# Masking inside the score operands, heads of a pair one after the other, staging in halves, narrow last blocks and a lag of 4 steps in an attention and feed-forward kernel

## The chip, the core and the metric

The kernel runs on one core of a Trainium2 chip. The metric is the device time of one execution in microseconds. The core has five engines that work side by side, each through its own queue in order: PE (TensorE, matrix multiply; the loading of its weights is listed apart as PEld), DVE (VectorE), ACT (ScalarE), POOL (GpSimd) and SP (SyncE), which here issues nearly all DMA transfers. SBUF is the on-chip memory, PSUM the memory that PE writes its results to. Partitions are the 128 rows of both.

## The reference

Block-causal attention over 8 batches, 8 heads, 576 positions and a head size of 64, and then a two-layer feed-forward part with a rational function between the layers:

```python
B, H, S, D = q.shape                        # 8, 8, 576, 64
scores = (1 / np.sqrt(D)) * np.matmul(q, k.transpose(0, 1, 3, 2))
mask = (pos[:, None] // 64) >= (pos[None, :] // 64)
scores = np.where(mask, scores, -1000000000.0)
scores = scores - np.max(scores, axis=-1, keepdims=True)
attn = np.exp(scores)
attn = attn / (np.sum(attn, axis=-1, keepdims=True) + 1e-09)
attn_out = np.matmul(attn, v)
x = attn_out.transpose(0, 2, 1, 3).reshape(B * S, H * D)       # 4608 x 512
h = x @ w_in                                                   # 512 x 2048
P = a[0] + a[1] * h + a[2] * h * h + a[3] * h * h * h
Q = 1.0 + np.abs(b[0]) * np.abs(h) + np.abs(b[1]) * h * h
out = (P / (Q + 1e-6)) @ w_out                                 # 2048 x 512
```

Everything is float32.

## The kernel before

**Precision by splitting.** Operands are split into a high part h, rounded to PE's reduced float32 type (F32R), and a low part l, the rest. A product is then two or three matmuls: h times h, h times l, l times h.

**Attention** goes over 32 pairs of heads (`visits`), each with five query tiles t of 64, 128, 128, 128, 128 rows (`NQ`, `Q0`). Tile t sees `NK[t]` = 64, 192, 320, 448, 576 keys, and only for its last 64 keys is part of the rows masked. The steps for a pair:

- `load` brings q, k, v of the pair; `prep(p, which)` transposes q (which = 0) and k (which = 1) on PE (L354, tile `tp`), in two halves of 288 positions each; ACT writes the high part (L358) and DVE the low part (L359) into one tile `hl` for q and k. When k is done, three transfers per head (L368 to L370) put the four parts into the operand tile `kq` of that head, 128 partitions high: head j's own 64 partitions hold qh, kh, kl and the other 64 hold ql, kh, kl. A product over 128 partitions therefore gives (qh + ql) times kh.
- `scores` (L402) makes the two matmuls of a piece (L420 with kh, L421 with kl, both with the same stationary operand) into a PSUM bank of pool `ps_a`, which has five banks. For t > 0 a third matmul (L424, 64 columns, operands `mrow` and `mcol`) adds -2^30 to the first 64 rows of the last 64 keys. DVE then takes the row maximum (L425).
- `expo` (L431) does the exponential with the row sum on ACT (L437). After the second head it normalises the tile: POOL adds 1e-9 to the sums (`rc`, L444), DVE inverts, POOL multiplies the first 64 keys of both heads into `pk` (L446) and the others in place (L450).
- `transp` (L454) transposes the normalised blocks of 64 x 2 or 128 keys on PE (L469); ACT and DVE split them into high and low tiles (`pt0`, `pt1`, `pt2`; L474, L475). `pv` (L478) multiplies them with the split v (L488): 5 blocks for the query tiles 0 to 2 and 9 blocks for 3 and 4, three matmuls per block, each 256 columns wide (320 for the first block). The result goes to memory (`xscr`, L493).

**Feed-forward** (class `Ffn`) works in chunks of 256 tokens and half the hidden units at a time: phase 0 (10 of 16 blocks of hidden units) runs between the steps of the attention, phase 1 behind it. A unit has 24 matmuls of 256 columns (L200), a chain on ACT, POOL and DVE (L207 to L233), and 12 matmuls of 512 columns (L249).

**The order of work.** `attn_steps` goes over a list `items` of (pair, tile, head), one per step and ten per pair; before the change the two heads of a tile follow each other: (t0, head 0), (t0, head 1), (t1, head 0) and so on. Each step puts its follow-ups at later steps: `expo` one step later (`ALAG2`), `transp` of a tile 9 steps after its second head's scores (`ALAG3` is 10, and one less than the distance to the same tile of the next pair is taken), `pv` a step after that, and for the next pair `load` at step 0, `prep` of q at step 3 and of k at step 5 (`OFFS`). After each step, units of feed-forward work are issued by a pace that starts at step 40 + `LAST`, `LAST` being `ALAG3` + 3. A list scheduler of the language then puts the instructions of each engine into a final order, by its own estimate of when they can run; that final order is what each engine's queue holds. A matmul that waits therefore holds up all that stands behind it on PE, and a transfer that waits holds up all behind it on SP.

The buffers around the change: `kq` has three tiles for the two heads of a pair (`KQB`), the probability tiles `p` one per query tile, `pk` two, `raw` q and k one each.

Of the kernel before, what the change touches and what calls it, by code (L numbers as in the profile page):

```python
# [29 lines left out]
KQB = 3  # L30
XB = 3
HOLD = 6
ALAG3 = 10
OFFS = {5:(0,3,5)}
# [24 lines left out]
def attn_ffn_kernel(  # L59
# [238 lines left out]
    with ExitStack() as actx:  # L298
# [5 lines left out]
        pt1 = [apers.tile([128, 4, 256], F32R, name=f"pt1{x}") for x in "hl"]  # L304
        pt2 = [apers.tile([128, 9, 256], F32R, name=f"pt2{x}") for x in "hl"]

        vpad = [apers.tile([128, 128 + 4 * 192], F32R, name=f"vp{x}") for x in "hl"]
        for x in pt1:
            nc.vector.memset(x[:, 2:4, 0:128].bitcast(F32), 0.0)
        for x in pt2:  # L310
            nc.vector.memset(x[:, 7:9, 0:128].bitcast(F32), 0.0)
        for x in vpad:
            nc.vector.memset(x.bitcast(F32), 0.0)

# [28 lines left out]
        def prep(p, which):  # L343

            s = st_[p]
            if which == 0:
                s["hl"] = att.tile([128, 4, S], F32R, name=f"hl{p}", tag="hl", bufs=1)
            raw, sc = (s["qr"], s["kr"])[which], (QSCALE, 1.0)[which]
            hl = s["hl"]
            h, l = (hl[:, 0], hl[:, 3]) if which == 0 else (hl[:, 1], hl[:, 2])  # L350
            for half in range(2):
                ps = bank(p - 1, f"tp{p}_{which}_{half}")[:, :3 * LP].rearrange("p (c t) -> p c t", c=3)
                for c in range(3):
                    nc.tensor.transpose(ps[:, c, :], raw[:, half * 3 + c].rearrange("p j d -> p (j d)"),  # L354
                                        ident[:LP, :LP])
                cs = slice(half * 288, half * 288 + 288)
                pf = ps.rearrange("p c t -> p (c t)")
                nc.scalar.activation(out=h[:, cs], in_=pf, func=AF.Copy, scale=sc)  # L358
                nc.vector.scalar_tensor_tensor(out=l[:, cs], in0=pf, scalar=sc, in1=h[:, cs].bitcast(F32),  # L359
                                               op0=ALU.mult, op1=ALU.subtract)  # L360
            if which == 1:


                for j in range(2):
                    kq = att.tile([128, 3, S], F32R, name=f"kq{p}_{j}", tag="kq", bufs=KQB)
                    src = hl[64 * j:64 * j + 64].bitcast(F32)
                    other = kq[64 - 64 * j:128 - 64 * j].bitcast(F32)
                    nc.sync.dma_start(out=kq[64 * j:64 * j + 64].bitcast(F32), in_=src[:, 0:3])  # L368
                    nc.sync.dma_start(out=other[:, 1:3], in_=src[:, 1:3])
                    nc.sync.dma_start(out=other[:, 0], in_=src[:, 3])  # L370
                    s["kq", j] = kq
# [30 lines left out]
        def scores(p, t, j):  # L402
            s = st_[p]
            nq = NQ[t]
            if j == 0:
                pt = att.tile([128, 2, NK[t]], F32, name=f"p{p}_{t}", tag=f"p{t}", bufs=1)

                pk = att.tile([128, 2, 64], F32, name=f"pk{p}_{t}", tag="pk", bufs=2) if t > 0 else pt
                nm = att.tile([128, 2, 2], F32, name=f"nm{p}_{t}", tag="nm", bufs=4)
                sm = att.tile([128, 2, 2], F32, name=f"sm{p}_{t}", tag="sm", bufs=4)  # L410
                s[t] = (pt, pk, nm, sm)
# [207 lines left out]
```

## Time and profile before

| | |
|---|---|
| three runs | 1387.34, 1393.5, 1398.72 us; median 1393.5 us |
| profiled execution, its own time | 1388.67 us |
| its span, first to last instruction | 1386.9 us |
| mean granted TensorE clock | 0.971 of full speed |
| busy: PE, PEld | 1296.0 us (93%), 1190.8 us (86%) |
| busy: DVE, ACT, POOL | 1031.0 (74%), 909.3 (66%), 958.3 us (69%) |
| DMA | 200.93 MB in 225635 packets, SP's queue 53.8% of 16 engines' span |
| feed-forward's matmuls, L200 and L249 | 25% and 25% of the chain that ended last |

How to read it: busy times of PE overlap between neighbouring matmuls, so the cost of one matmul is read from the distance of the starts and not from its duration. A row of the table by stretches gives the stretch, its length, the busy time of PE, PEld, DVE, ACT and POOL with the number of instructions, the granted clock, the share of the DMA engines and GB/s. A row of waits gives the engine and the line that waited, what it waited for, the total in us, how often, and the longest.

### The profile page before, as it was taken

The numbers are of one execution on the slowest core, as the hardware profiler recorded it, in microseconds if no ns is written. First come the engines' busy times: TensorE is split into PE (matmuls) and PEld (weight loads), VectorE is DVE, ScalarE is ACT, GpSimd is POOL, SyncE is SP. The second block draws the span as 40 slices with busy tenths as digits, with TensorE's granted clock in tenths as the row PEclk, the third lists the DMA queues.
The fourth block names the chain that finished last, engine by engine and source line by source line (L and its number), as shares of the span: only waits on it lengthen the run. The fifth ranks groups of instructions, "written<-read, shape, count | busy, mean of one in ns | idle before, by whom it ended". The sixth has DMA issues, their size and how long they took to land.

```text
span 1386.9 us, 25820 instructions
## 1 busy us (share of the span) xinstructions
PE 1296.0 (93%) x8736; PEld 1190.8 (86%) x8736; DVE 1031.0 (74%) x2048; ACT 909.3 (66%) x2250; POOL 958.3 (69%) x1240
## 2 busy tenths in 40 slices
PE   4778799999899989999999999999989999999998
PEld 3667788999888889888989999999979999999897
DVE  5898877787678868877767777766756677777665
ACT  5766766777577766776777777776545655555553
POOL 4888987687677757777767676766556655556564
PEclk9687999999999999999999999999999999999999
DMA  9778555666556665675654565651711333333332
GB/s 221 191 195 236 147 150 160 168 168 181 147 136 154 163 167 140 156 171 140 168 134 110 153 149 126 150 141 44 263 55 61 107 122 122 122 122 122 122 122 91
DMA packets 225635, 200.93 MB, mean 145 GB/s; under 512 B 132064, under 2 KB 195552, under 8 KB 225504
## 3 DMA queue, kind: packets, MB, share of 16 engines
q1 hardware_dynamic: 225440, 199.28, 53.8%
q8 instruction: 70, 1.15, 0.3%
q14 instruction: 61, 0.50, 0.1%
q0 software_dynamic: 64, 0.00, 0.0%
HBM read 98.57 MB, written 44.04 MB: 103 GB/s over the span
## 4 chain that ended last, share of the span: by engine, by line
PE 70%; DVE 9%; POOL 8%; ACT 5%; DMA 4%; issue 2%; SPq 1%; POOLq 0%; ACTq 0%; DVEq 0%
PE h L200 25%; PE o L249 25%; PE o L488 9%; PE t L469 4%; PE s L420 3%; PE s L421 3%; PE tp L354 2%; ACT p L437 1%; DVE v L224 1%; POOL u L210 1%; DVE nm L425 1%; POOL p L450 1%; DMA x<-xscr 1%; POOL gl L233 1%; DVE u L223 1%
## 5 line engine op out<-in xcount | busy, mean ns | idle before, releaser
L200 PE MATMUL h<-x,wih 128*128 128x256 f32 x2304 | 442.6, 288 | 10.1 <-DMA x<-xscr 5.9
L200 PEld LDWEIGHTS h<-x,wih 128*128 128x128 f32 x2304 | 368.8, 192 | 19.6 <-issue 6.8
L200 PE MATMUL h<-x,wil 128*128 128x256 f32 x1152 | 329.5, 286 | 0.0
L249 PE MATMUL o<-woh,gl 128*128 128x512 f32 x576 | 233.0, 405 | 8.1 <-POOL gl L233 6.8
L209 POOL TENSOR_SCALAR v<-u,bab 128x512 f32<-128x512 f32 x144 | 119.7, 831 | 162.9 <-ACT u L207 160.8
L249 PE MATMUL o<-woh,gh 128*128 128x512 f32 x576 | 228.5, 397 | 0.0
L249 PE MATMUL o<-wol,gh 128*128 128x512 f32 x576 | 227.2, 395 | 0.0
L233 POOL TENSOR_TENSOR gl<-s,gh 128x512 fp32r<-128x512 f32 x144 | 188.4, 1309 | 51.4 <-ACT gh L232 48.3
L425 DVE TENSOR_REDUCE nm<-s 128x1 f32<-128x288 f32 (+4 forms) x384 | 161.7, 427 | 81.2 <-PE s L424 46.1
L200 PEld LDWEIGHTS h<-x,wil 128*128 128x128 f32 x1152 | 221.3, 192 | 0.5
L437 ACT ACTIVATE p<-s,nm 128x288 f32<-128x288 f32 (+4 forms) x384 | 184.6, 485 | 48.4 <-DVE nm L425 34.9
L210 POOL TENSOR_TENSOR u<-v,u 128x512 f32<-128x512 f32 x144 | 189.7, 1318 | 9.8
L450 POOL TENSOR_SCALAR p<-p,rc 128x128 f32<-128x128 f32 (+3 forms) x256 | 166.2, 660 | 30.0 <-DVE rc L445 28.3
L217 ACT ACTIVATE v<-u,qcb 128x512 f32<-128x512 f32 x144 | 104.6, 726 | 95.9 <-POOL u L210 95.1
L207 ACT ACTIVATE u<-h 128x512 f32<-128x512 f32 x144 | 86.0, 597 | 120.8 <-PE h L200 114.4
L420 PE MATMUL s<-kq 128*128 128x256 f32 (+3 forms) x384 | 138.3, 362 | 22.0 <-DMA kq<-hl 9.6
L211 DVE TENSOR_TENSOR s<-s,h 128x512 f32<-128x512 f32 x144 | 98.6, 684 | 68.7 <-ACT s L208 67.9
L249 PEld LDWEIGHTS o<-woh,gl 128*128 128x128 f32 x576 | 109.5, 190 | 28.9 <-POOL gl L233 9.3
L249 PEld LDWEIGHTS o<-wol,gh 128*128 128x128 f32 x576 | 109.1, 189 | 22.8
L249 PEld LDWEIGHTS o<-woh,gh 128*128 128x128 f32 x576 | 109.5, 190 | 16.0
L421 PE MATMUL s<-kq 128*128 128x256 f32 (+3 forms) x384 | 121.0, 317 | 0.0
L469 PE MATMUL t<-ident,p 128*128 128x128 f32 (+1 forms) x672 | 114.0, 280 | 6.2 <-DVE x L492 1.8
(105 smaller groups left out, 3031.9 us busy)
## 6 DMA issues: line engine op xcount, KB each, us to landing
kq<-hl SPq DMA_DIRECT2D x64, 432.0 KB, 4.2
x<-xscr SPq DMA_DIRECT2D x96, 256.0 KB, 3.6
kq<-hl SPq DMA_DIRECT2D x64, 288.0 KB, 5.3
xscr<-x SPq DMA_DIRECT2D x32, 320.0 KB, 4.2
qr<-in_q_dram SPq DMA_DIRECT2D x64, 144.0 KB, 2.8
kr<-in_k_dram SPq DMA_DIRECT2D x64, 144.0 KB, 2.9
kq<-hl SPq DMA_DIRECT2D x64, 144.0 KB, 4.8
pscr<-os SPq DMA_DIRECT2D x18, 512.0 KB, 3.2
```

The lines of the kernel that those rows point to most:

```text
L200: nc.tensor.matmul(h[:, j, :], lhsT=w[:, dc, fs], rhs=xs[dc // 2][:, dc % 2, hl, :], start=(dc == 0 and i == 0), stop=(dc == 3 and i == 2))
L209: nc.gpsimd.tensor_scalar(out=vt, in0=ut, scalar1=b1, scalar2=b0, op0=ALU.mult, op1=ALU.add)
L210: nc.gpsimd.tensor_tensor(out=ut, in0=vt, in1=ut, op=ALU.mult)
L233: nc.gpsimd.tensor_tensor(out=gl.rearrange("p j t -> p (j t)"), in0=st, in1=gh.rearrange("p j t -> p (j t)").bitcast(F32), op=ALU.subtract)
L249: nc.tensor.matmul(self.o[m], lhsT=g[:, j, ms], rhs=w[:, f, :], start=(u == 0 and j == 0 and i == 0), stop=(u == nu - 1 and j == 1 and i = ...
L420: nc.tensor.matmul(ps[:, :ww], lhsT=kq[:, 0, qs], rhs=kq[:, 1, c0:c0 + ww], start=True, stop=False)
L421: nc.tensor.matmul(ps[:, :ww], lhsT=kq[:, 0, qs], rhs=kq[:, 2, c0:c0 + ww], start=False, stop=not last)
L425: nc.vector.reduce_max(out=nm[:nq, j, i:i + 1], in_=ps[:nq, :w], axis=AX.X, negate=True)
L437: nc.scalar.activation(out=pt[:nq, j, c0:c0 + w], in_=banks[i][:nq, :w], func=AF.Exp, bias=nm[:nq, j, 0:1], scale=1.0, accum_out=sm[:nq, j ...
L450: nc.gpsimd.tensor_scalar(out=pt[:nq, jj, 64:n], in0=pt[:nq, jj, 64:n], scalar1=rc[:nq, jj:jj + 1], scalar2=1.0, op0=ALU.mult, op1=ALU.mult)
L469: nc.tensor.transpose(ps[:, i, :nq], src, ident[:nq, :nq])
L488: nc.tensor.matmul(o[:, s0:w], lhsT=vblock(vv, x), rhs=pp, start=(x == 0 and i == 0), stop=(x == nb - 1 and i == 2))
```

## The change

The operand tile `kq` gets a fourth plane, and the two score matmuls get a stationary and a moving operand each. The first pairs (qh, mask row part) with (kh, mask column part): the head's own 64 partitions hold qh and kh, and the other 64 hold two mask planes, which are built once on POOL, written to memory (`mscr`) and copied from there into each `kq`. The second pairs (qh, ql) with (kl, kh). The matmul with `mrow` and `mcol` is gone; the product ql times kl, which the two matmuls before included, is gone too.

`items` puts the five tiles of head 0 ahead of the five of head 1. `prep` does one half of q or k at a time, at steps 5, 6, 7 and 8, with `load` at step 3; each half has an `hl` tile of its own (two buffers) and its own transfers: four per half of q or k, and one per head for the mask planes, so 18 per pair in place of 6. `ALAG3` is 4 and always holds, so `LAST` is 7 in place of 13.

The last two blocks of each `pv` get tiles of their own (`pt3`, `pt4`), 128 columns wide, so that their matmuls are 128 wide in place of 256. The transposes of query tile 0 use all 128 rows of a tile `p0` with zeros in its lower half; those of tile 4 are grouped 4, 3, 2 in place of 3, 3, 3, and the copy and subtraction of tile 2's four blocks are split in two. `pk` has four buffers, and the maxima a tile per head.

```diff
-ALAG3 = 10
-OFFS = {5:(0,3,5)}
+ALAG3 = 4
+OFFS = {5:(3,5,6,7,8)}
...
-    mrow = cpool.tile([128, 128], F32R, name="mrow")
-    mcol = cpool.tile([128, 64], F32R, name="mcol")
...
-        pt1 = [apers.tile([128, 4, 256], F32R, name=f"pt1{x}") for x in "hl"]
-        pt2 = [apers.tile([128, 9, 256], F32R, name=f"pt2{x}") for x in "hl"]
+        pt1 = [apers.tile([128, 2, 256], F32R, name=f"pt1{x}") for x in "hl"]
+        pt2 = [apers.tile([128, 7, 256], F32R, name=f"pt2{x}") for x in "hl"]
+        pt3, pt4 = ([apers.tile([128, 2, 128], F32R, name=f"pt{i}{x}") for x in "hl"] for i in (3, 4))
+        p0 = apers.tile([128, 2, 64], F32, name="p0")
+        nc.vector.memset(p0[64:128], 0.0)
...
+        mscr = dpool.tile([64, 2, S], F32, name="mscr")
+        mask = ffn.tile([64, 2, S], F32, name="mask", tag="os")
...
+        nc.sync.dma_start(out=mscr, in_=mask)
...
-        def prep(p, which):
+        def prep(p, which, half):
...
+            if which == 0 and half == 0:
                 for j in range(2):
-                    kq = att.tile([128, 3, S], F32R, name=f"kq{p}_{j}", tag="kq", bufs=KQB)
-                    src = hl[64 * j:64 * j + 64].bitcast(F32)
-                    other = kq[64 - 64 * j:128 - 64 * j].bitcast(F32)
-                    nc.sync.dma_start(out=kq[64 * j:64 * j + 64].bitcast(F32), in_=src[:, 0:3])
-                    nc.sync.dma_start(out=other[:, 1:3], in_=src[:, 1:3])
-                    nc.sync.dma_start(out=other[:, 0], in_=src[:, 3])
+                    kq = s["kq", j] = att.tile([128, 4, S], F32R, name=f"kq{p}_{j}", tag="kq", bufs=KQB)
+            hl = att.tile([128, 2, 288], F32R, name=f"hl{p}_{which}_{half}", tag="hl", bufs=2)
...
+                if which == 0:
+                    if half == 0:
+                        nc.sync.dma_start(out=other[:, 0:3:2], in_=mscr)
+                    nc.sync.dma_start(out=own[:, 0:2, cs], in_=src[:, 0:1].to_broadcast([64, 2, 288]))
+                    nc.sync.dma_start(out=other[:, 1, cs], in_=src[:, 1])
+                else:
+                    nc.sync.dma_start(out=own[:, 2:4, cs], in_=src)
+                    nc.sync.dma_start(out=other[:, 3, cs], in_=src[:, 0])
...
-                nc.tensor.matmul(ps[:, :ww], lhsT=kq[:, 0, qs], rhs=kq[:, 1, c0:c0 + ww], start=True, stop=False)
-                nc.tensor.matmul(ps[:, :ww], lhsT=kq[:, 0, qs], rhs=kq[:, 2, c0:c0 + ww],
-                                 start=False, stop=not last)
-                if last:
-                    nc.tensor.matmul(ps[:, w - 64:w], lhsT=mrow, rhs=mcol, start=False, stop=True)
+                nc.tensor.matmul(ps[:, :ww], lhsT=kq[:, 0, qs], rhs=kq[:, 2, c0:c0 + ww], start=True, stop=False)
+                nc.tensor.matmul(ps[:, :ww], lhsT=kq[:, 1, qs], rhs=kq[:, 3, c0:c0 + ww], start=False, stop=True)
...
-                    nc.tensor.transpose(ps[:, i, :nq], src, ident[:nq, :nq])
+                    nc.tensor.transpose(ps[:, i, :], src, ident)
...
+                pt, b0, s0 = (((pt2, x, 0) if x < 7 else (pt4, x - 7, 128)) if g else
+                              (pt0, 0, 0) if x == 0 else (pt1, x - 1, 64) if x < 3 else (pt3, x - 3, 192))
...
-        items = [(i, t, j) for i, (_, ts) in enumerate(visits) for t in ts for j in range(2)]
+        items = [(i, t, j) for i, (_, ts) in enumerate(visits) for j in range(2) for t in ts]
...
-                            at(k + o1, prep, p + 1, 0)
-                            at(k + o2, prep, p + 1, 1)
+                            for i, o in enumerate(o1):
+                                at(k + o, prep, p + 1, i // 2, i % 2)
...
-                        lag = min(ALAG3, nxt[k] - 1)
+                        lag = ALAG3
```

What moves in the engines' queues is seen at three places. A name such as `s_4_1_0` is the score tile of query tile 4, head 1, piece 0; `tp_1_0` is the staging transpose of k, half 0; `t_1_0` is the first group of transposed blocks of tile 1; `h` and `o` with the `wih` and `woh` operands are feed-forward matmuls.

PE before, from the staging transposes of the next pair's k to that pair's first score, about half way through the attention (some 100 more rows lie in the gaps):

```order
L354 MATMUL tp_1_0_5079<-ident,kr_4859 128x96 x3
L354 MATMUL tp_1_1_5085<-ident,kr_4859 128x96 x3
L488 MATMUL o_0_5059<-pt1l,vph 128x256
...
L420 MATMUL s_3_0_0_5146<-kq_0_4625 128x448
L421 MATMUL s_3_0_0_5146<-kq_0_4625 128x448
L424 MATMUL s_3_0_0_5146<-mcol,mrow 128x64
...
L420 MATMUL s_4_1_1_5280<-kq_1_4629 128x288
L421 MATMUL s_4_1_1_5280<-kq_1_4629 128x288
L424 MATMUL s_4_1_1_5280<-mcol,mrow 128x64
...
L469 MATMUL t_0_0_5307<-ident,p_0_4869 128x64
...
L420 MATMUL s_0_0_0_5334<-kq_0_5091 128x256
```

PE after the change, the whole stretch from the transposes of k's half 0 to the score of the next pair that needs them, in a pair about as far on:

```order
L364 MATMUL tp_1_0_6444<-ident,kr_6212 128x96 x3
L428 MATMUL s_2_1_0_6463<-kq_1_5880 128x320
L429 MATMUL s_2_1_0_6463<-kq_1_5880 128x320
L364 MATMUL tp_1_1_6468<-ident,kr_6212 128x96 x3
L428 MATMUL s_3_1_0_6487<-kq_1_5880 128x448
L429 MATMUL s_3_1_0_6487<-kq_1_5880 128x448
L478 MATMUL t_0_0_6508<-ident,p_132 128x128
L428 MATMUL s_4_1_0_6521<-kq_1_5880 128x288
L429 MATMUL s_4_1_0_6521<-kq_1_5880 128x288
...
L478 MATMUL t_1_1_6534<-ident,p_1_6124 128x128 x2
L428 MATMUL s_0_0_0_6551<-kq_0_6321 128x256
```

The left-out rows are the second piece of tile 4 (two matmuls of 288) and `t_1_0`. Where a whole pair's matmuls stood between the transposes of k and the score that reads them, 15 matmuls stand there now.

SP before, the staging of one pair, with other transfers between:

```order
L370 DMA kq_0_6439<-hl_6344 64x576
L334 DMA qr_6663<-in_q_dram 96x6x64 x2
L368 DMA kq_0_6439<-hl_6344 64x1728
L369 DMA kq_0_6439<-hl_6344 64x1152
L493 DMA xscr_76<-x_0_6423 128x2x320
...
L368 DMA kq_1_6443<-hl_6344 64x1728
L369 DMA kq_1_6443<-hl_6344 64x1152
L370 DMA kq_1_6443<-hl_6344 64x576
```

SP after the change, the transfers of q's second half and of k's first half of one pair:

```order
L379 DMA kq_0_6321<-hl_0_1_6378 64x2x288
L380 DMA kq_0_6321<-hl_0_1_6378 64x288
L379 DMA kq_1_6322<-hl_0_1_6378 64x2x288
L380 DMA kq_1_6322<-hl_0_1_6378 64x288
L382 DMA kq_0_6321<-hl_1_0_6443 64x2x288
L383 DMA kq_0_6321<-hl_1_0_6443 64x288
L382 DMA kq_1_6322<-hl_1_0_6443 64x2x288
L383 DMA kq_1_6322<-hl_1_0_6443 64x288
```

Six large transfers became sixteen small ones and two of the mask, which follow each other directly.

POOL before, around the normalisation of the query tiles 3 and 4 of one pair and 0 of the next:

```order
L443 TENSOR_TENSOR sm_4_8376<-sm_4_8376 128x2
L446 TENSOR_TENSOR pk_3_8317<-p_3_8316,rc_3_8367 128x128
L444 TENSOR_SCALAR rc_4_8483<-sm_4_8376 128x2
L450 TENSOR_SCALAR p_4_8373<-p_4_8373,rc_4_8483 128x512 x2
L444 TENSOR_SCALAR rc_0_8544<-sm_0_8503 64x2
L446 TENSOR_TENSOR p_0_8501<-p_0_8501,rc_0_8544 64x128
L446 TENSOR_TENSOR pk_4_8374<-p_4_8373,rc_4_8483 128x128
L209 TENSOR_SCALAR v_8_2_9235<-u_8_2_9234,bab 128x512
```

POOL after the change, the query tiles 2 to 4 of one pair:

```order
L455 TENSOR_TENSOR pk_2_8795<-p_2_8506,rc_2_8796 128x128
L459 TENSOR_SCALAR p_2_8506<-p_2_8506,rc_2_8796 128x256 x2
L139 TENSOR_TENSOR wpo_4_9274<-wpo_4_9274,wao_4_9272 128x512
L455 TENSOR_TENSOR pk_3_8831<-p_3_8543,rc_3_8832 128x128
L459 TENSOR_SCALAR p_3_8543<-p_3_8543,rc_3_8832 128x384 x2
L452 TENSOR_TENSOR sm_4_8630<-sm_4_8630 128x2
L453 TENSOR_SCALAR rc_4_8860<-sm_4_8630 128x2
L455 TENSOR_TENSOR pk_4_8859<-p_4_8629,rc_4_8860 128x128
L459 TENSOR_SCALAR p_4_8629<-p_4_8629,rc_4_8860 128x512 x2
L227 TENSOR_TENSOR gl_8_2_9716<-s_8_2_9402,gh_8_2_9715 128x512
```

The normalisations of the tiles follow each other with little between, where the two heads in turn spread them over the pair.

More of the change, by code (lines that the diff above doesn't have):

```diff
@@ new lines, in prep @@
+            if which == 0 and half == 0:
+                for j in range(2):
+                    kq = s["kq", j] = att.tile([128, 4, S], F32R, name=f"kq{p}_{j}", tag="kq", bufs=KQB)
+            hl = att.tile([128, 2, 288], F32R, name=f"hl{p}_{which}_{half}", tag="hl", bufs=2)
+            h, l = hl[:, 0], hl[:, 1]
+            ps = bank(p - 1, f"tp{p}_{which}_{half}")[:, :3 * LP].rearrange("p (c t) -> p c t", c=3)
+            for c in range(3):
+                nc.tensor.transpose(ps[:, c, :], raw[:, half * 3 + c].rearrange("p j d -> p (j d)"),
+                                    ident[:LP, :LP])
@@ new lines, in prep @@
+            cs = slice(half * 288, half * 288 + 288)
+            pf = ps.rearrange("p c t -> p (c t)")
+            nc.scalar.activation(out=h, in_=pf, func=AF.Copy, scale=sc)
+            nc.vector.scalar_tensor_tensor(out=l, in0=pf, scalar=sc, in1=h.bitcast(F32),
+                                           op0=ALU.mult, op1=ALU.subtract)
+            for j in range(2):
+                kq = s["kq", j]
+                src = hl[64 * j:64 * j + 64].bitcast(F32)
+                own = kq[64 * j:64 * j + 64].bitcast(F32)
+                other = kq[64 - 64 * j:128 - 64 * j].bitcast(F32)
+                if which == 0:
[6 more added lines that the diff above has]
+                    nc.sync.dma_start(out=other[:, 3, cs], in_=src[:, 0])
@@ L405, in scores @@
             if j == 0:
[L406 to L411, printed above, removed]
-            pt, pk, nm, sm = s[t]
+                pt = att.tile([128, 2, NK[t]], F32, name=f"p{p}_{t}", tag=f"p{t}", bufs=1) if t > 0 else p0
+                sm = att.tile([128, 2, 2], F32, name=f"sm{p}_{t}", tag="sm", bufs=6)
+                s[t] = (pt, sm)
+            nm = s["nm", t, j] = att.tile([128, 2], F32, name=f"nm{p}_{t}_{j}", tag="nm", bufs=4)
             kq = s["kq", j]
@@ L433, in expo @@
             nq, n = NQ[t], NK[t]
[L434 removed]
+            pt, sm = s[t]
+            nm = s.pop(("nm", t, j))
             banks = s.pop((t, j))
@@ L454, in transp @@
         def transp(p, t):
-            pt, pk, _, _ = st_[p].pop(t)
+            pt, pk = st_[p].pop(t)
             nq = NQ[t]
             nb = 1 + 2 * t
-            groups = {1: [1], 3: [1, 2], 5: [1, 4], 7: [4, 3], 9: [3, 3, 3]}[nb]
+            groups = {1: [1], 3: [1, 2], 5: [1, 4], 7: [4, 3], 9: [4, 3, 2]}[nb]
             blk = 0
@@ L483, in pv @@
             for x in range(nb):
-                s0 = 64 if (g == 0 and x > 0) else 0
-                hi, lo = ((y[:, x] for y in pt2) if g else (y[:, 0] for y in pt0) if x == 0 else
-                          (y[:, x - 1] for y in pt1))
+                pt, b0, s0 = (((pt2, x, 0) if x < 7 else (pt4, x - 7, 128)) if g else
+                              (pt0, 0, 0) if x == 0 else (pt1, x - 1, 64) if x < 3 else (pt3, x - 3, 192))
+                hi, lo = (y[:, b0] for y in pt)
                 for i, (vv, pp) in enumerate(((vh, lo), (vh, hi), (vl, hi))):
@@ L493, in pv @@
             nc.sync.dma_start(out=xscr[b][:, hp, :, g * 320:g * 320 + w], in_=xs[:, :, :w].bitcast(F32))
-        items = [(i, t, j) for i, (_, ts) in enumerate(visits) for t in ts for j in range(2)]
-        nxt = [next((n - k for n in range(k + 1, len(items)) if items[n][1:] == items[k][1:]), 99)
-               for k in range(len(items))]
+        items = [(i, t, j) for i, (_, ts) in enumerate(visits) for j in range(2) for t in ts]
         def attn_steps():
@@ L538, in attn_ffn_kernel @@
             next(wsteps)
-        prep(0, 0)
-        prep(0, 1)
+        for x in range(4):
+            prep(0, x // 2, x % 2)
         vprep(0)
```

65 lines of the change are left out of this document (27 added, 38 removed).

## The prediction

> **What bounds the kernel now.** I read the busy time of each engine by stretch first, since an average over the program mixes stages.
>
> ```profile
> 35.00:70.00 35.00, 26.03 (x138) 22.53 (x138) 29.18 (x73) 24.71 (x75) 30.68 (x40) 0.70 0.74 191
> ...
> 300.00:400.00 100.00, 93.27 (x654) 86.86 (x653) 76.78 (x164) 70.33 (x190) 73.33 (x102) 0.97 0.61 159
> ...
> 700.00:800.00 100.00, 98.24 (x715) 92.01 (x714) 72.67 (x162) 72.56 (x196) 66.69 (x104) 1.00 0.56 139
> ...
> 1050.00:1386.00 336.00, 331.43 (x2088) 299.58 (x2087) 230.41 (x328) 182.85 (x295) 197.29 (x175) 1.00 0.36 113
> ```
>
> The columns are PE, PEld, DVE, ACT, POOL, granted clock, DMA share, GB/s. Early on POOL is the fullest engine (30.68 of 35 us) and PE gets a clock of 0.70. From about 200 us PE sets the pace: 93 to 98 of 100 us, the others near 73. The last 336 us are feed-forward alone, which the change does not touch. So PE work removed counts from 200 us on, which holds 25 of the 32 pairs. But PE takes its matmuls in order and is nearly full only because hardly anything in its queue is late:
>
> ```profile
> PE s L420 <- DMA kq<-hl: 9.6, 4, 4.7
> ```
>
> ```profile
> SPq L184 <- PE h L200: 233.2, 28, 14.9
> ```
>
> In the whole run PE waits four times, 9.6 us, for the staged operand kq. The second row is the DMA queue of SP: it also works in order, and stands 233.2 us behind loads whose buffer is not yet free. Today nobody pays for that.
>
> **The change part by part.** *Mask matmuls.* The cost of one is read from starts, since matmuls overlap:
>
> ```profile
> 830.49 0.37 PE L421 MATMUL s<-kq 128*128 128x448 f32 x1
> 830.70 0.19 PE L424 MATMUL s<-mcol,mrow 128*128 128x64 f32 x1
> 830.73 0.36 PE L200 MATMUL h<-x,wil 128*128 128x256 f32 x1
> 830.93 0.40 PE L200 MATMUL h<-x,wih 128*128 128x256 f32 x2
> 831.16 0.28 PE L200 MATMUL h<-x,wil 128*128 128x256 f32 x1
> ...
> 842.02 0.28 PE L488 MATMUL o<-pt2l,vph 128*128 128x256 f32 x1
> 842.14 0.28 PE L488 MATMUL o<-pt2h,vph 128*128 128x256 f32 x1
> ```
>
> A 256-wide matmul starts 0.12 us after its like (842.02, 842.14). From the mask matmul to the second start behind it are 0.23 us (830.70 to 830.93), of which 0.12 belong to the 256-wide one: the mask costs 0.11. There are 32 pairs x 2 heads x 4 query tiles = 256: 28 us. The two remaining matmuls per piece load weights as often as before (384 loads on each line), so folding the mask in adds no PE work.
>
> *Transpose of tile 0.* Today it uses 64 rows:
>
> ```profile
> 829.84 0.49 PE L469 MATMUL t<-ident,p 128*128 128x128 f32 x3
> 830.08 0.36 PE L200 MATMUL h<-x,wih 128*128 128x256 f32 x1
> 830.29 0.37 PE L420 MATMUL s<-kq 128*128 128x448 f32 x1
> ...
> 843.36 0.19 PE L424 MATMUL s<-mcol,mrow 128*128 128x64 f32 x1
> 843.48 0.27 PE L469 MATMUL t<-ident,p 64*128 64x64 f32 x1
> 843.68 0.39 PE L420 MATMUL s<-kq 128*128 128x256 f32 x1
> 843.90 0.28 PE L421 MATMUL s<-kq 128*128 128x256 f32 x1
> ```
>
> It starts 0.12 after the mask matmul where others start 0.03 after it (0.09 lost), and 0.42 pass to the second start behind it: 0.09 + 0.42 less the 0.12 of L420 is 0.39 in all. Full-height transposes take (0.45 - 0.12)/3 = 0.11 (829.84 to 830.29). The change pads to full height: 0.28 x 32 = 9 us.
>
> *Narrow blocks.* Four of fourteen blocks of P times V go from 256 to 128 columns, 2 x 3 x 2 x 32 = 384 matmuls. No 128-wide matmul of this type is in the trace. The lower bound is the transposes' 0.11; the upper is the mask row taken as a rate, 0.11 for 64 columns, so 0.22 for 128. I take 0.11, since a 64-column matmul and a 128-column transpose cost the same, which looks like a floor under each matmul: 0.01 x 384 = 4 us gained. By the upper bound it is 38 us lost. The Trainium skill (TensorE: Matmul & The Clock Gate, LDWEIGHTS) puts a weight load at its columns over 1.2 ns, an estimate of 107 ns for 128 columns whatever the moving width; the mask row agrees, and the 96-wide transposes (x6 in 0.66 us, below), with 128 weight columns and some 0.08 apart, do not. By it the term would be 5 us instead of 4.
>
> Together 41 us of PE work, of which 25/32 = **-32 us** lie where PE bounds.
>
> *Staging in halves, sequence and offsets.* One pair's staging today:
>
> ```profile
> 825.42 0.66 PE L354 MATMUL tp<-ident,kr 96*128 96x96 f32 x6
> ...
> 826.60 0.73 ACT L358 ACTIVATE hl<-tp 128x288 fp32r<-128x288 f32 x2
> ...
> 827.63 0.81 DVE L359 SCALAR_TENSOR_TENSOR hl<-tp,hl 128x288 fp32r<-128x288 f32 x2
> ...
> 828.47 0.49 SPq L368 DMA_DIRECT2D kq<-hl  x1
> ...
> 829.00 0.60 SPq L369 DMA_DIRECT2D kq<-hl  x1
> ```
>
> The DMA issues (KB of one, median us from issue to landing), and the landings of all kq transfers:
>
> ```profile
> qr<-in_q_dram SPq DMA_DIRECT2D x64, 144.0 KB, 2.8
> ...
> kq<-hl SPq DMA_DIRECT2D x64, 144.0 KB, 4.8
> ```
>
> ```profile
> DMA to landing us min/median/max: 2.3/4.8/8.9
> ```
>
> From the end of the transposes (826.08) to the first issue are 2.4 us, to the second issue 0.5 more, then the landing: 4.8 by the 144 KB row of the same transfer. That is 7.7 us. Before, the first score of the next pair starts at 843.68, so 10 us are to spare. In the new order only a handful of PE rows stand between the key transposes of half 0 and the score that needs them (the PE order shown with the change). At the spacings of this trace (320 columns 0.15, 448 0.20, 288 0.13, 256 0.12, 512 0.23, transposes 0.11, staging ones 0.08) the short form adds up to 1.9 us. Adding up every pair from 200 us on in that way gives 1.9 for seven pairs, 4.7 to 5.7 for ten, and over 6 for eight; before, it was 14 to 21. The chain itself is shorter with halves: one copy and one subtraction instead of two of each (0.4 + 0.4), a smaller transfer. Lower bound: 1.1 to the first issue, 0.5, 2.8 as the 144 KB load lands: 4.4 us. Upper: 7.7. I take the middle, 6.1, since the copies queue behind other work of ACT and DVE (0.5 us each above) and four transfers of the query half are issued just ahead, at 0.5 us each. PE then stands 7 x 4.2 + 10 us = **+39 us** (17 at 4.4, 72 at 7.7). Behind the waiting score queue the transposes, P times V and feed-forward matmuls. The query half's own buffer (two for four halves) lets the key half be copied only once the query transfers have read it; that falls in the same place, and I leave it in the upper bound.
>
> *Lag 4.* Transposes now come close behind the normalisation on POOL (groups of 200 to 900 us):
>
> ```profile
> L210 POOL TENSOR_TENSOR u<-v,u 128x512 f32<-128x512 f32 x63 | 82.3, 1306 | 3.5
> ...
> L446 POOL TENSOR_TENSOR pk<-p,rc 128x128 f32<-128x128 f32 x92 | 45.3, 493 | 32.4 <-PE t L469 30.6 <-DVE rc L445 0.5
> ...
> L450 POOL TENSOR_SCALAR p<-p,rc 128x512 f32<-128x512 f32 x46 | 35.0, 773 | 3.7 <-DVE rc L445 3.5
> L450 POOL TENSOR_SCALAR p<-p,rc 128x384 f32<-128x384 f32 x45 | 32.0, 724 | 5.8 <-DVE rc L445 4.3 <-PE o L488 1.0 <-PE t L469 0.4
> ```
>
> Heads in sequence make four normalisations come in one burst: tiles 3 and 4 alone are 2 x 0.49 + 2 x 0.72 + 2 x 0.77 = 4.0 us, with feed-forward work of 1.3 us apiece between. The same adding-up, POOL rows against PE rows, leaves the transposes 12 to 19 us of slack before (medians by tile) and 0 to 3 now, with ten of the 25 pairs 1 to 3 us late. Much of it falls in pairs where PE already stands for kq: **+8 us** (0 to 16).
>
> *Clock.* At 93% busy the row of 300 us has 0.97, at 98% that of 700 has 1.00. With 47 us of waits in 750 us PE falls to about 93%: 1 to 1.5% of it, **+8 us** (0 to 12). The Trainium skill (same page, the HAM clock gate) halves the clock after an idle window of about 3.4 us; seven waits of 4.2 us would each cost an estimated 1.7 us, 12 instead of 8, and a sum of 1414.
>
> *Feed-forward six steps earlier* (its start is tied to the lag): dense stepping places 0.56 half-units a step, each about 2.9 us (24 x 0.12), so 6 x 0.56 x 2.9 = 10 us move into a stage with PE room, but POOL has little (30.68 of 35): **-5 us** (-10 to 0). *Start:* the mask is built on POOL, written and read back before the first score; PE's early rows have slack, the chain less: **+3 us** (0 to 15). Twelve more DMA issues a pair are 6 us of SP, inside the chain above; the split copy of tile 2 (one more on ACT and DVE) fits under their 70 to 77%.
>
> Sum: -32 + 39 + 8 + 8 - 5 + 3 = +21 on the profiled execution, 1388.7 (span 1386.9 and 1.8 around it; the median of three runs shown is 1393.5): **1410 us**. Its own range, from the ends of the kq term, is 1385 to 1445.
>
> **The rivals.** *A, faster:* the small transfers land at the minimum row, 2.3, and the copies run at once: a chain of 3.9, PE stands 7 x 2.0 = 14 us, POOL and clock cost nothing: -32 + 14 - 5 = -23, **1366**. It decides below a chain of about 4.2. For it: halves of 72 and 144 KB. Against: 4.8 for the same size today. *B, break-even:* the lower bound 4.4 and half of the POOL and clock terms: -32 + 17 + 8 - 5 + 2, **1379**. *C, narrow matmuls at the mask's rate:* 42 us dearer than in my sum, 25/32 of it in the PE stage: **1443**. For it: the mask row alone allows it. Against: the transposes. *That the mask would not go away* is excluded by the order: no mask matmul is left.
>
> **How the numbers follow.** Forecast 0.44, A 0.26, B 0.16, C 0.14. Faster by over 1% takes 0.22 of A and half of B, which lies on the line: 0.30. Within 1%, about what a measurement of this kernel can tell from no change, are 0.04 of A, 0.08 of B and 0.10 of the forecast: 0.22. Slower by over 1%: 0.34 of the forecast and C, 0.48. The range 1358 to 1462 reaches to A and C.
>
> **What would show it.** Right: waits of PE's scores for kq of 20 us or more, tens of times; no L424 row; 128-wide P times V at 0.11 spacing; PE busy about 93% from 300 to 900 us. Wrong: kq waits under 15 us with PE at 97%, or a 128-wide spacing near 0.2, or the time lost before 200 us.

## The result, and the profile after

The changed kernel takes **1501.4 us** (1493.05 to 1504.4), the kernel before 1391.0 in the same comparison: a ratio of **1.079 (1.076 to 1.082)**, slower. The profiled execution took 1499.1 us, with a span of 1497.4 and a clock of 0.942.

The table by stretches of the changed kernel (PE, PEld, DVE, ACT, POOL, granted clock, DMA share, GB/s):

```profile
0.00:200.00 200.00, 124.71 (x693) 106.50 (x694) 141.07 (x330) 119.90 (x348) 130.44 (x194) 0.80 0.76 196
...
35.00:70.00 35.00, 23.76 (x139) 20.24 (x138) 23.55 (x60) 21.04 (x63) 24.21 (x35) 0.74 0.90 228
300.00:400.00 100.00, 91.48 (x625) 83.47 (x625) 70.46 (x146) 65.83 (x171) 69.50 (x91) 0.97 0.57 155
500.00:600.00 100.00, 86.22 (x552) 76.71 (x551) 67.87 (x152) 62.58 (x176) 60.89 (x92) 0.90 0.57 155
700.00:800.00 100.00, 90.11 (x598) 81.58 (x597) 71.47 (x155) 64.89 (x177) 65.76 (x97) 0.93 0.51 136
```

Before, the first 200 us held 147.23 us of PE work in 896 instructions, as one row of the same table says:

```profile
0.00:200.00 200.00, 147.23 (x896) 132.78 (x897) 163.04 (x372) 134.16 (x385) 160.79 (x218) 0.86 0.75 192
```

Every engine does less per stretch, in the first 200 us (124.71 of PE instead of 147.23) as well as later: in the rows shown PE has 86 to 91 of 100 us where it had 93 to 98. No other engine took over; POOL, the fullest of the others early on, fell from 30.68 to 24.21 of 35 us. The feed-forward stage behind the attention did not change. The last pieces of the last scores, from the timelines of the kernel before and of the changed one:

```profile
960.89 0.29 PE L421 MATMUL s<-kq 128*128 128x288 f32 x1
```

```profile
1074.32 0.29 PE L429 MATMUL s<-kq 128*128 128x288 f32 x1
```

Behind them are 426 us before (1386.9 less 961) and 423 now: the attention alone grew by 113 us. What PE, ACT and SP wait for (engine, line, what for, us, times, longest), in rows of the kernel before and then of the changed one:

```profile
PE tp L354 <- DMA kr<-in_k_dram: 4.5, 4, 1.7
...
ACT hl L358 <- DMA kq<-hl: 3.8, 1, 3.8
...
PEld t L469 <- POOL p L450: 3.2, 5, 1.1
...
PEld t L469 <- POOL pk L446: 2.2, 2, 1.2
```

```profile
PE tp L364 <- DMA kr<-in_k_dram: 30.3, 15, 4.5
...
PE s L428 <- DMA kq<-hl: 11.4, 9, 2.4
PE s L428 <- DVE hl L369: 11.0, 11, 2.7
...
PEld t L478 <- POOL p L459: 23.4, 25, 2.8
...
PEld t L478 <- POOL pk L455: 14.2, 11, 3.3
...
ACT hl L368 <- DMA kq<-hl: 37.0, 27, 8.7
...
SPq L378 <- PE s L429: 97.6, 20, 10.3
```

The scores wait for kq 9 times, 11.4 us, hardly more than the 9.6 of before. The new waits stand elsewhere: transposes of k for k's load, weight loads of the transposes for POOL, and ACT for an `hl` buffer that the q transfers still read. SP stands at the mask transfers (L378), whose `kq` tile is read by the pair at work. And the transfers landed far sooner than before (KB of one, median us to landing; then the landings of all transfers into kq):

```profile
kq<-hl SPq DMA_DIRECT2D x256, 144.0 KB, 2.5
...
kq<-hl SPq DMA_DIRECT2D x256, 72.0 KB, 2.1
kq<-mscr SPq DMA_DIRECT2D x64, 288.0 KB, 4.0
...
DMA to landing us min/median/max: 1.9/2.4/8.4
```

One pair's staging shows how these waits follow from each other (start, duration, engine, and in brackets the idle time before and who ended it):

```profile
240.33 0.42 PE L364 MATMUL tp<-ident,qr 96*128 96x96 f32 x3
...
241.61 1.08 SPq L344 DMA_DIRECT2D kr<-in_k_dram  x2
...
243.28 0.65 SPq L379 DMA_DIRECT2D kq<-hl  x1
...
245.81 0.44 PE L364 MATMUL tp<-ident,kr 96*128 96x96 f32 x3 [3.01 <-DMA kr<-in_k_dram]
...
246.66 0.59 SPq L380 DMA_DIRECT2D kq<-hl  x1
...
246.79 0.41 ACT L368 ACTIVATE hl<-tp 128x288 fp32r<-128x288 f32 x1 [2.69 <-DMA kq<-hl]
...
247.35 0.54 SPq L383 DMA_DIRECT2D kq<-hl  x1
...
252.83 0.60 SPq L383 DMA_DIRECT2D kq<-hl  x1
```

q and k share one raw buffer, before and after the change: both are made by one line with the tag `raw` and `bufs=1`. (The text on the kernel before gives one to each; that was a misreading.) So k can be loaded only when the second half of q has been transposed, 240.33. In the change one step lies between the two, and PE stands 3.01 us. Behind k's load SP issues the staging transfers one after the other, some 0.68 us each (from 243.28 to 246.66 are five such steps). ACT stands 2.69 us at the copy of k's half, and with it whatever is behind it on ACT. The profile puts this down to the buffer, as the release that came last; but k's transposes end only at 246.25, so k's late load has the larger part here and the buffer the last 0.5 us. Over the whole run it is the other way round: of ACT's 37.0 us of such waits, 28.3 lie behind the end of the transposes. k's last transfer of the pair is issued 12.5 us after q's last transposes start.

The 11.0 us put down to DVE's subtraction are not waits for `kq` at all:

```profile
429.22 0.42 PE L364 MATMUL tp<-ident,kr 96*128 96x96 f32 x3
...
430.29 0.41 ACT L368 ACTIVATE hl<-tp 128x288 fp32r<-128x288 f32 x1 [0.56 <-PE tp L364]
...
433.26 0.44 DVE L369 SCALAR_TENSOR_TENSOR hl<-tp,hl 128x288 fp32r<-128x288 f32 x1
...
433.85 0.37 PE L428 MATMUL s<-kq 128*128 128x288 f32 x1 [2.73 <-DVE hl L369]
```

This score of tile 4 belongs to the pair at work, whose operands have long been there. The staging transposes take PSUM banks of the same pool, and DVE starts to empty the bank 2.6 us after ACT's copy of it has ended (430.70).

The 128-wide matmuls of P times V:

```profile
825.84 0.27 PE L504 MATMUL o<-pt4h,vph 128*128 128x128 f32 x1
825.96 0.28 PE L504 MATMUL o<-pt4h,vpl 128*128 128x128 f32 x1
826.07 0.28 PE L504 MATMUL o<-pt4l,vph 128*128 128x128 f32 x1
826.18 0.28 PE L504 MATMUL o<-pt4h,vph 128*128 128x128 f32 x1
826.29 0.27 PE L504 MATMUL o<-pt4h,vpl 128*128 128x128 f32 x1
```

0.45 us for four steps, 0.11 apiece: the value that the prediction took.

### The profile page after: what moved, and what is told of

Read it like the earlier page. It is cut to its first block, busy times and chain, and to the rows that moved or that the text cites. A ratio compares the mean times of both kernels' runs of the same rounds, so it can differ in the third digit from the quotient of the medians.

```text
span 1497.4 us, 26243 instructions
## 1 busy us (share of the span) xinstructions
PE 1311.3 (88%) x8480; PEld 1179.8 (79%) x8480; DVE 1041.5 (70%) x2073; ACT 919.2 (61%) x2282; POOL 959.4 (64%) x1245
## 4 chain that ended last, share of the span: by engine, by line
PE 54%; POOL 7%; DVE 6%; DMA 6%; ACT 4%; issue 2%; SPq 2%; ACTq 0%; DVEq 0%; POOLq 0%
PE o L243 21%; PE h L194 20%; PE o L504 6%; PE t L478 3%; DMA kq<-hl 3%; DMA x<-xscr 2%; PE s L428 2%; PE s L429 1%; POOL u L204 1%; POOL p L459 1%; POOL v L203 1%; POOL gl L227 1%; ACT p L443 1%; DMA kr<-in_k_dram 1%; PE tp L364 1%
## 5 line engine op out<-in xcount | busy, mean ns | idle before, releaser
L243 PE MATMUL o<-woh,gl 128*128 128x512 f32 x576 | 238.1, 414 | 15.4 <-POOL gl L227 13.5
L243 PE MATMUL o<-woh,gh 128*128 128x512 f32 x576 | 234.1, 406 | 0.0
L243 PE MATMUL o<-wol,gh 128*128 128x512 f32 x576 | 232.1, 403 | 0.0
L428 PE MATMUL s<-kq 128*128 128x256 f32 (+3 forms) x384 | 144.2, 381 | 40.9 <-DMA kq<-hl 11.4
L243 PEld LDWEIGHTS o<-woh,gl 128*128 128x128 f32 x576 | 114.2, 198 | 39.7 <-POOL gl L227 17.8
L478 PE MATMUL t<-ident,p 128*128 128x128 f32 x672 | 122.2, 296 | 19.0 <-POOL p L459 10.5
L243 PEld LDWEIGHTS o<-wol,gh 128*128 128x128 f32 x576 | 113.0, 196 | 24.9
L394 POOL TENSOR_TENSOR vpl<-vr,vph 128x256 fp32r<-128x256 f32 (+1 forms) x128 | 77.7, 615 | 81.3 <-ACT vph L393 58.3
L243 PEld LDWEIGHTS o<-woh,gh 128*128 128x128 f32 x576 | 113.7, 197 | 18.3
```

Source lines behind the costliest of these rows:

```text
L243: nc.tensor.matmul(self.o[m], lhsT=g[:, j, ms], rhs=w[:, f, :], start=(u == 0 and j == 0 and i == 0), stop=(u == nu - 1 and j == 1 and i = ...
L428: nc.tensor.matmul(ps[:, :ww], lhsT=kq[:, 0, qs], rhs=kq[:, 2, c0:c0 + ww], start=True, stop=False)
L478: nc.tensor.transpose(ps[:, i, :], src, ident)
```

## The experiments

Theory: the time goes to waits that staging and the short lag bring. Rivals: the order of the heads itself, the early start of the feed-forward work, or the mask planes and the many small transfers. After each time stand its ratio to the kernel before and the interval of the ratio. The medians of the kernel before beside these runs were 1388.8 to 1392.6 us, so kernels timed beside different runs of it compare to about 4 us.

**Staging, within the changed kernel.** Its SBUF is full; a third `hl` buffer needed room, so there is a control with the room alone.

```diff
-OFFS = {5:(3,5,6,7,8)}
+OFFS = {5:(3,5,5,7,8)}        # b1: both halves of q in one step
```

> Both halves of q are staged at step 5, k's at 7 and 8 as in the change, so that two steps instead of one lie between q's last transposes and k's first. q and k share one raw buffer, so k's load can only start when q's transposes are done. Theory R (k's load is late): PE's wait for the load of k (30.3 us, 15 times) falls below 12 us and the time by 20 to 35 us, to about 1470. Theory H (the ring of two staging buffers stops ACT): ACT's wait for the kq transfers stays near 37 us and the time within 10 us of 1500. Theory K (kq itself lands late, as predicted): no change, 1500.

Measured 1493.7 (1.0746, 1.0730 to 1.0762). PE's wait for k's load fell from 30.3 to 17.0 us, ACT's for the `hl` buffers rose to 41.1 from 37.0. The time fell by 8 us where theory R expected 20 to 35.

```diff
-tag="pk", bufs=4
+tag="pk", bufs=2              # b4, also in b2 and b3
-mask = ffn.tile([64, 2, S], F32, name="mask", tag="os")
+m0, m1 = (ffn.tile([64, S], F32, name=f"mask{i}", tag="os") for i in range(2))
...
-tag="hl", bufs=2
+tag="hl", bufs=3              # b2
...
+qr, kr = ([att.tile([LP, 3, 2, D], F32, name=f"{n}r{p}_{i}", tag="raw", bufs=3) for i in range(2)]
+          for n in "qk")      # b3, in place of one raw buffer
```

> Control: only the room is made (two pk buffers in place of four, the mask built as two tiles), nothing else. All theories: within 8 us of 1500. If the normalisation on POOL is what counts (theory B: it comes in a burst and close ahead of the transposes), fewer pk buffers show as 10 us or more on top.

> Three staging buffers hl in place of two; the room comes from two pk buffers in place of four and a mask built as two tiles. Theory H: ACT's wait for kq transfers (37.0 us, 27 times, up to 8.7) falls below 10 us, DVE's wait for hl (25.4) with it, and the time by 30 to 60 us, to about 1455. Theory R: PE's wait for k's load stays and the time moves by less than 12 us. Theory K: PE's wait for kq (11.4 us) would have to carry it, no change.

> q and k are loaded in halves into three raw buffers of half the size, so k's first half is loaded without waiting for q's transposes; same room as the run with three staging buffers, four more DMA issues per pair. Theory R: PE's wait for the load of k nearly vanishes (30 to below 8 us) and the time falls by 20 to 35 us, to about 1470. Theories H and K: within 10 us of 1500.

Measured: control 1491.2 (1.0722, 1.0706 to 1.0738); third buffer 1482.9 (1.0664, 1.0647 to 1.0681); raw in halves 1496.4 (1.0757, 1.0738 to 1.0775). The control alone is 10 us below the changed kernel, so fewer `pk` buffers did not cost anything, and the 8 us of b1 and the 8 us from the control to the third buffer are no more than a rebuild with little in it moves. The waits, too, are to be compared with the control's, where PE's for k's load is 19.2 us and ACT's for `hl` 29.8. With the third buffer ACT's fell to 19.3 and PE's for k's load rose to 32.5. Raw in halves took PE's to 6.4, ACT's went to 60.6 in 46 waits, and the time is 5 us above the control: the waits moved and did not go away. Inside the changed order none of these buffers is the cause by itself.

**With room.** To change more, 8 blocks of feed-forward instead of 10 run beside the attention (`NFA = 8`), in both kernels, which frees SBUF for four `kq` and four `hl` tiles:

```diff
-NFA = 10
+NFA = 8          # d1: kernel before; d2: changed; all below
-KQB = 3
+KQB = 4          # e3, and d4, d3 below
-tag="hl", bufs=2
+tag="hl", bufs=4
...
-OFFS = {5:(3,5,6,7,8)}
+OFFS = {5:(0,2,3,5,6)}        # d4: staging earlier
...
-items = [(i, t, j) for i, (_, ts) in enumerate(visits) for j in range(2) for t in ts]
+items = [(i, t, j) for i, (_, ts) in enumerate(visits) for t in ts for j in range(2)]
-ALAG3 = 4
+ALAG3 = 10       # d3: heads in turn, lag 9 as before, OFFS (0,3,3,5,5)
```

> Control for the next three: the kernel before, with 8 instead of 10 of the 16 hidden blocks in phase 0 (16 KB of SBUF come free during the attention, the feed-forward work that leaves it is done in phase 1). Same PE work in all. All theories: 1390 to 1420 us, since some fill for the attention's waits is moved away.

> Control: the changed kernel with 8 hidden blocks in phase 0. The waits of the changed attention have less work to cover them: 1500 to 1530 us.

> The changed kernel with 8 hidden blocks in phase 0, four kq tiles and four staging buffers, but load and staging at steps 3, 5, 6, 7, 8 as in the change (the run with four kq tiles and early staging has 0, 2, 3, 5, 6). Theory L (buffers are what counts: the loop over kq and the ring): about 1500, as that run. If it is the time of the staging, that is the distance from the staging to the scores that read it: 1535 or more, near the control of the changed kernel (1557).

> The changed kernel with heads in sequence and lag 4, 8 hidden blocks in phase 0, but four kq tiles and four staging buffers, and staging at steps 2, 3, 5, 6 with the load at 0: the staging no longer waits for the last scores of the pair's first head and is three steps earlier. Theory L (the loop over kq: the next pair's staging starts only behind the fourth tile's scores and its own scores behind that): 50 us or more below the changed kernel's control. Theory S (sequence and lag themselves, through the normalisation on POOL just ahead of the transposes): within 25 us of that control.

> The changed kernel's PE work (mask inside the operands, narrow blocks, full-height transposes of tile 0) and its staging in halves with 18 transfers, but heads interleaved as before, lag 10 (9 in effect), staging at steps 3 and 5; 8 hidden blocks in phase 0 to make room for four kq tiles and four staging buffers. Theory S (the sequence of heads and the lag of 4 that goes with it are the loss): 20 to 40 us below the control of the kernel before, as the PE work counts now. Theory M (the mask planes, the many small transfers or halves are the loss): still 60 us or more above that control. Theories H and R: in between.

Measured: d1 1443.1 (1.0369, 1.0340 to 1.0399), d2 1556.9 (1.1187, 1.1154 to 1.1221), e3 1534.3 (1.1051, 1.1020 to 1.1081), d4 1489.8 (1.0710, 1.0685 to 1.0736), d3 1426.2 (1.0247, 1.0214 to 1.0279). Both controls missed their forecasts by 23 us or more: moving two blocks out of the attention costs each kernel 50 to 56 us. The 114 us between d2 and d1 are close to the 110 at 10 blocks, so the ladder (a row of runs, each one step from the last, from d1 to d2) is taken to stand for the change; only the totals show that. In d4 staging has room and time, and the transposes wait for POOL:

```profile
PEld t L478 <- POOL p L459: 28.6, 62, 1.5
PEld t L478 <- POOL pk L455: 22.0, 23, 3.3
```

In d3 the first of these rows is hardly there:

```profile
PEld t L478 <- POOL p L459: 2.9, 5, 1.0
```

d3 is 17 us below its control d1. It has the mask planes, the halves and the 18 transfers of the change, so with room and the old order these are not the loss. What separates d4 from d3 was lag and order together; so one more run changes only the lag, with the start of the feed-forward work held:

```diff
-ALAG3 = 10
+ALAG3 = 4        # g1: d3 with lag 4
-LAST = ALAG3 + 3
+LAST = 13
```

> The version with the mask inside, interleaved heads, four kq and four hl tiles, 8 blocks (1426), with the lag set to 4 and the start of the feed-forward pace left where it was. If the short lag is what made the sequence version 64 us slower, this one comes at 1475 to 1490 with tens of waits of the transposes for POOL. If the sequence of the heads is the cause (four normalisations in one burst), it stays at 1425 to 1440.

Measured 1481.7 (1.0651, 1.0614 to 1.0689): 55 us for the edit of the lag alone, heads still in turn. In the profiles the last score starts 40 us later than in d3 (955.7 against 915.7); the rest lies behind the attention. The waits of d4 are back:

```profile
PEld t L478 <- POOL p L459: 24.1, 42, 2.0
PEld t L478 <- POOL pk L455: 23.7, 19, 5.5
```

The order of the heads shows no large cost of its own: d4, in sequence, is 8 us from g1. That is the sum of three changes, with the earlier feed-forward start and other offsets, which no run separates. But the order forces the lag. There is one `p` tile per query tile; in turn, the next pair writes it nine steps after the second head's score, in sequence five.

**The lag in the kernel before**, where nothing else is new.

```diff
-ALAG3 = 10
+ALAG3 = 4        # e1;  g3: 4 and LAST = 13;  g2: 7 and LAST = 13
```

> The kernel before with one number changed: the lag to the transposes is 4 steps in place of 10 (9 in effect), the heads interleaved, everything else as it was. Theory G (the short lag costs by itself: the transposes stand right behind the normalisation on POOL, with PE's queue behind them): PE waits for POOL's pk and p at the transposes, 40 us or more in sum, and the time is 25 to 60 us above 1390. Theory Q (it is the sequence of heads, through the burst on POOL and the loop over kq, and not the lag): within 12 us of 1390, or below it, as the feed-forward work starts six steps earlier.

> The kernel before with a lag of 4, but the start of the feed-forward pace left at 13. If the 52 us of the earlier run with lag 4 come from the lag itself, 1436 to 1446 again. If they come from feed-forward work starting six steps earlier, in the stretch where POOL is the fullest engine, 1390 to 1400.

> The kernel before with a lag of 7, the start of the feed-forward pace left at 13. If slack shrinks step by step and the waits are of one kind, about half of what lag 4 costs: 1410 to 1420. If there is a point below which the normalisation is late and above which nothing is, 1390 to 1398.

Measured: e1 1441.1 (1.0368, 1.0346 to 1.0390), g3 1422.9 (1.0241, 1.0211 to 1.0271), g2 1408.2 (1.0121, 1.0095 to 1.0147). So lag 9, 7, 4 cost 0, 19, 34 us: the cost grows with each step of slack that is gone, and these points show no lag above which it is nothing. In g3 the last score starts 42 us later than in the kernel before (1002.5 against 960.9), as the lag cost 40 in g1. POOL is not the only wait that grows. PE also waits longer for kq, 23.6 us in g2 and 19.2 in g3, where the kernel before had 9.6 (g3):

```profile
PE s L420 <- DMA kq<-hl: 19.2, 8, 7.4
```

The other 18 us of e1 go with the feed-forward work that starts six steps earlier with the lag, by which the prediction had gained 5. The stretch where they differ most, in e1 and then in g3:

```profile
140.00:200.00 60.00, 39.62 (x240) 35.78 (x239) 54.30 (x106) 41.01 (x106) 53.94 (x61) 0.80 0.56 152
```

```profile
140.00:200.00 60.00, 52.36 (x353) 47.80 (x352) 47.25 (x107) 43.51 (x118) 46.08 (x60) 0.94 0.50 129
```

With the early start POOL and DVE are at 90% there, and PE does 13 us less; over the first 200 us it does 7.6 less (135.20 against 142.83). A full POOL alone does not explain it, as the kernel before has 53.28 of POOL in the same 60 us with 52.14 of PE. So the 18 us are measured, and how they arise is not shown.

**PE work alone, in the kernel before.** e2 takes the narrow last blocks and full-height transposes from the change, g4 the transposes alone.

```diff
-nc.tensor.transpose(ps[:, i, :nq], src, ident[:nq, :nq])
+nc.tensor.transpose(ps[:, i, :], src, ident)       # g4; e2 with pt3, pt4 as in the change
```

> The kernel before with only the narrow last blocks (384 matmuls of 128 in place of 256 columns) and the full-height transposes of tile 0; mask matmuls, order, lag and staging as before. By the terms of the prediction, 4 + 9 us of PE work, of which 25/32 count: 10 us faster, 1380. If the 128-wide matmuls cost 0.22 us apiece: 20 to 30 us slower. If PE's work hardly counts because waits fill what is freed: within 4 us of 1390.

> The kernel before with only the transposes of query tile 0 made full height (32 x 0.28 = 9 us less PE work). If PE work removed from the stage where PE sets the pace counts, 1383 (25/32 of 9). If PE gains nothing because another limit (the pace of feed-forward units, set at build time, and waits that grow by as much) holds the time, 1389 to 1392.

Measured: e2 1391.0 (1.0004, 0.9987 to 1.0021), g4 1389.7 (0.9994, 0.9975 to 1.0013). 13 and 9 us of PE work less, and no gain. Both have their matmuls in a new order, with more waits for kq than the 9.6 us of before (e2, then g4); in g4 the 2.3 us more are only a part of what is missing:

```profile
PE s L419 <- DMA kq<-hl: 18.1, 6, 5.8
```

```profile
PE s L422 <- DMA kq<-hl: 11.9, 5, 6.8
```

h1 starts the feed-forward work six steps later in the kernel before, h2 does so with e2's edit:

```diff
-LAST = ALAG3 + 3
+LAST = 19
```

> The kernel before with its lag of 10, the feed-forward pace starting six steps later (19 in place of 13). Starting it six steps earlier cost 18 us in the kernel with lag 4 (1441 against 1423). If that is a matter of what feed-forward work does to POOL in the stretch before 200 us, starting later wins something or nothing: 1375 to 1391. If the 18 us belong to lag 4 only, or if the later start only moves units into a stage where PE is full: 1390 to 1410.

> The same with the narrow last blocks and the full-height transposes of the change (13 us less PE work). If PE work removed counts once the early stretch is out of the way, 5 to 12 us below the other kernel of this call. If it is given back in waits again, the same time within 3 us.

Measured: h1 1385.4 (0.9962, 0.9941 to 0.9982), h2 1415.3 (1.0178, 1.0159 to 1.0198). h1 is the only one of these kernels below the kernel before, by 0.4%. h2 does 13 us less PE work than h1 and is 30 us slower; its second matmuls of feed-forward wait for POOL (h1, then h2):

```profile
PE o L249 <- POOL gl L233: 4.1, 8, 1.2
```

```profile
PE o L249 <- POOL gl L233: 20.8, 14, 6.0
```

Why the narrow blocks end there was not settled. A rebuild of this kernel with a small edit can thus move by 30 us, as far as is known through its order alone, and a single difference of 10 to 20 us between two builds proves little. That holds for g2's 19 us, the 18 us of the early start and the smaller steps of the ladder too. The lag of 4, in two kernels, and the 45 us of the staging steps are larger than any of these.

**The best of the change at 10 blocks.** f1 puts d3's order into the changed kernel with three `hl`, two `pk` and three `kq` tiles, `OFFS` (0,3,3,5,9).

```diff
-OFFS = {5:(3,5,6,7,8)}
+OFFS = {5:(0,3,3,5,9)}        # f1; items and ALAG3 as in d3
```

> All 10 hidden blocks in phase 0: the changed kernel's operands (mask inside, narrow blocks, full height, staging in halves) with the heads interleaved and lag 10 as before; three kq tiles, three staging buffers, two pk, staging at steps 3, 3, 5 and 9, so that the last half waits for the kq tile that comes free at step 8. If the gain of the same idea with 8 blocks carries over (1426 against 1443): about 1373 to 1380. If the staging through three buffers holds up ACT as in the change: 1400 or more.

Measured 1451.0 (1.0425, 1.0393 to 1.0456). With three `kq` tiles the last half of k comes late:

```profile
PE s L429 <- DMA kq<-hl: 19.5, 6, 10.0
```

50 us of the change's 110 come back, but not the rest; d3's buffers do not fit beside 10 blocks. No version with the mask inside that beats the kernel before was found.

## Why the prediction was wrong

The ladder at 8 blocks, where every step is a run, against the terms of the sum:

| step | measured, us | the prediction's term |
|---|---|---|
| d1 to d3: mask inside, narrow blocks, transposes, halves | -17 | -32 |
| d3 to g1: lag 4 | +55 | +8 |
| g1 to d4: heads in sequence, earlier feed-forward, offsets | +8 | -5 |
| d4 to e3: staging later, steps 3 to 8 | +45 | +39, with the next |
| e3 to d2: three `kq`, two `hl` | +23 | in the upper bound |
| clock, start | inside the others | +8, +3 |
| together | +114 | +21 |

**The step that failed is the lag**, "+8 us (0 to 16)". The reasoning compared the end of POOL's rows with the transposes and charged only what came out late, at most 3 us in ten pairs. The direction was right (transposes do wait for POOL, 23.4 and 14.2 us), but the slack of 12 to 19 us before was not spare: with the lag at 4 it cost 34 us in the kernel before and 55 on the ladder. The likely reason is that in that stage the engines run at 67 to 98%, each queue in order, and slack lets one fall behind without stopping the others. How the 34 us divide among the single waits was not shown. The direct waits of the transposes' weight loads for POOL in g3 come to 24 us, where the kernel before had 5, and PE's waits for kq to 10 more:

```profile
PEld t L469 <- POOL p L450: 13.3, 25, 1.4
...
PEld t L469 <- POOL pk L446: 10.8, 10, 5.1
```

**The staging term lay inside its bounds for the wrong reason** (45 and 23 us together, against 39, 17 to 72). It was to be a chain of copy, issue and landing at which the scores stand, "waits of PE's scores for kq of 20 us or more, tens of times". They were 9, of 11.4 us, and the chain's landing, taken at 2.8 to 4.8, was 2.4. By the first half of the prediction's own test ("kq waits under 15 us") the mechanism fell. The second half, PE at 97%, did not come: PE was at 86 to 91%, with other waits in their place. So rival A did not win either: it had the landing right and missed the time by 135 us. The loss sits ahead of the chain and beside it: the shared raw buffer, SP's sixteen issues in a row, the `hl` ring ("falls in the same place": it does not, it stands on ACT), the PSUM banks, and staging that begins late. Of these only steps (45) and buffers (23) were separated by runs. The landing bound came from the 144 KB rows of a kernel with other traffic. The Trainium skill (SBUF — State Buffer, The DMA setup-cost knee) gives 2 us and the bytes over 436 GB/s, an estimate of 2.2 us for 72 KB and 2.3 for 144; here the rows of 2.1 and 2.5 agree, and the 4.8 of before, for the same 144 KB, does not.

**PE work removed** was costed right in itself (0.11 for the narrow matmuls, no mask row left, so rival C is excluded) and overrated in time. In the kernel before, 9 and 13 us less gave 0; in d3, where the whole saving is in, 17 of 32. "PE work removed counts from 200 us on" held in full in none of them; in e2, g4 and h2 other waits grew, which is a likely reason and not a shown one.

**The clock** was sized too small. Its mean fell from 0.971 to 0.942: in the records of the granted clock PE has half speed for 80 us before and for 174 now. Counting in these stretches the matmuls that end 1.6 to 2.4 times the median spacing of their shape behind the end before, there are 237 before, with 23 us above that spacing, and 392 now, with 47. So an estimate of +24 stands against +8 (0 to 12). It is no separate step of the ladder, since the waits and the clock come together: in the same stretches the longer gaps between matmuls grew from 29 to 83 us.

**Feed-forward earlier**, -5, has the wrong sign: it cost 18 us in e1 against g3, and the later start of h1 gained 4. That the stretch at 35 to 70 us is short of POOL was seen, and taken as a limit to a gain instead of a cost. The first 200 us, named as a way to be wrong, have their share: 22.5 us less PE work is done there. But the loss is not gathered there. The first score of the eighth pair (24 score matmuls a pair) starts at 218.5 in place of 199.0, 19.5 of the 113 us for 7 of the 32 pairs.

The prediction's own range was added up loosely as well: with 17 and 72 for the kq term its sum gives 1388 and 1443, where it has 1385 and 1445.

## What to carry to other kernels

In a kernel whose engines are all at two thirds or more with in-order queues, slack between stages is a resource: shortening a lag from 9 to 4 steps cost 34 and 55 us where adding up the queues gave 8, so price a lost step of slack by a run with that step alone. Look for what a new order forces (here heads in sequence force the short lag through single `p` buffers) and for buffers shared by a tag before costing a chain. Removing a few us of PE work in a list-scheduled kernel (one whose instructions are put into a new order at each build) is not to be counted as a gain until the new order's waits are seen: here it was worth nothing twice and 17 of 32 us once.

## What the runs showed of the hardware

- Matmuls of this type do not get cheaper below about 128 columns: 64 wide (0.11 us before) and 128 wide (0.11 after) cost the same, 256 wide 0.12. It is no floor for every instruction, as the 96-wide staging transposes follow each other in 0.08.
- The small transfers land in 2.1 (72 KB) and 2.5 us (144 KB). Before, a 144 KB transfer into the same tile took 4.8. SP needs some 0.68 us to issue each; for sixteen in a row that makes an estimate of 11 us whatever their landing.
- The granted clock is at half speed in stretches of 3.4 us and multiples of it (up to 17.1 in the changed kernel). A mean of 0.90 from 500 to 600 us, 20.5 us at half speed, cost an estimated 6.4 us by the count above, and PE stood in longer gaps for 5.8 of them.
